# Threshold attention and a hard-swish MLP on one core: idle transposes, the relay of the score bursts, the spread of the block transposes, and the last slot's output tile

## The chip, the cores and the metric

The kernel runs on one core of a Trainium2 chip. The metric is the device time of one execution in microseconds (us). Three runs of the kernel before the change gave 502.87, 503.57 and 503.82, a median of 503.57. A separate, profiled execution is what all rows of the profile come from; its own time is given below.

The engines are named as in the profile: PE is the tensor engine (PEld its weight loads), DVE the vector engine, ACT the scalar engine, POOL is GpSimd, SP is the sync engine, which only issues DMAs and waits.

## The reference

```python
# q, k, v: (batch 8, heads 8, sequence 576, head width 64) float32, tau = 0.02
scores = q @ k.T / 8
scores = where(scores >= max(scores, -1) - tau, scores, -1e9)
attn   = softmax(scores)            # over the keys
a      = attn @ v                   # (8, 8, 576, 64)
x      = a.transpose(0, 2, 1, 3).reshape(4608, 512)
h      = x @ w_in                   # w_in: 512 x 2048
g      = h * clip(h + 3, 0, 6) / 6
out    = g @ w_out                  # w_out: 2048 x 512, out: 4608 x 512 float32
```

Attention keeps only the keys whose score lies within tau of the row's maximum; the result, laid out token by token, goes through a two-layer MLP.

## The kernel before, in words

**Slots.** The attention is cut into 144 slots, 18 for each of 8 batches (`queue`). A slot is 128 query rows of two heads. A "quad" is half of a batch's heads (4 heads), 16 quads in all. For each quad the kernel loads `nq` and `nk` (queries and keys, 576 KB each) and turns them into `qT` and `kT` with block transposes on DVE: `transpose_k` in two parts (two instructions each, L111) and `transpose_q` in two parts (one instruction each, L97). `nat_pool` keeps two buffers, so a quad's load waits until the transposes of the quad two before it have read the old one.

**One slot's softmax.** PE multiplies the scores into PSUM, for two slots together, in a `burst` (L218). DVE's `sm_max` (L232, two instructions a slot) copies them to SBUF as tile `s` and takes the row maxima; POOL makes a bias of them (L241); ACT masks (`sm_mask`, L246) and exponentiates with a row sum (`sm_exp`, L251), two instructions each; DVE takes the reciprocal (L254); POOL scales into `pn` (`sm_norm`, L259). `pn` is then transposed, for the first 10 slots by PE with copies by DVE (`pe_transpose`, L279 to L281), for all later ones by a DMA transpose on SP's queue (L270). `av` (L288) multiplies by v, a DVE copy (L296) makes `xT`, `mm1` (L311) multiplies by `w_in`, `mm1_relu` (ACT L329 or DVE L331) and `mm1_gate` (DVE L344) make g, and `mm2_part` (L311) multiplies by `w_out` in four parts a tile of 128 tokens; `mm2_out` (L363 on DVE, L361 on ACT) scales it and the output DMA goes out.

**PSUM.** There is one PSUM tile of 8 banks, divided by hand. The scores of two consecutive slots lie in banks 0 to 5 and overlap in one bank, so a burst can start only when `sm_max` has read the pair before. Banks 6 and 7 (`HB`, `OB`) serve `mm1` and `mm2`, and `pe_transpose` in the first slots.

**The relay.** Inside a burst the last products of the second slot must not start before an earlier one has ended. The wait goes over a `nop` on another engine: it waits for the matmul and releases the next ones.

```python
            if step is None:
                relay = by.nop()
                behind(relay, mm)
                continue
```

Engines work in the order of the program, so whatever stands behind the `nop` on the engine `by` waits too. In the lead-in (slots 0 to 13, two slots a cycle, loop over `n = 0, 2, ... 12`) `by` is POOL for the first cycle and DVE for the others; later it is POOL.

**Order.** Everything is written out by hand (`manual_schedule`); each engine works strictly through its own list. `at(jobs, n, ...)` puts a block transpose behind slot n's work on DVE, `at(issues, n, ...)` an input DMA at the end of slot n. Quads 2 and 3 are loaded by SP, later ones by POOL. After the lead-in each slot does its softmax, one `mm1` item, and from slot 21 on (`N2`) each odd slot two parts of `mm2` (`second()`). Behind the last slot comes the tail: `rest1` runs the `mm1` items that are left over four PSUM banks (0, 3, 2, 5 in turn), `rest2` the `mm2` tiles that are left, then come the last four `av` products, their eight `mm1` items and two more `mm2` tiles, the second in two halves (`last_tile`, L575, L578).

**Idle transposes.** `warm_up(count)` (L156) makes PE transpose an identity matrix `count` times into PSUM that nobody reads. It stands before the first burst (24), behind it (6), behind the next ones (10, then 3 a cycle) and in a few early slots (4).

Of the kernel before, what the change touches and what calls it, by code (L numbers as in the profile page):

```python
# [9 lines left out]
F32 = mybir.dt.float32  # L10
# [5 lines left out]
P = 128  # L16
# [4 lines left out]
def kernel(  # L21
# [10 lines left out]
    nc = tc.nc  # L32
    B, H, S, D = q.shape
# [6 lines left out]
    N1, N2 = 14, 21  # L40
    HB, OB = 6, 7
    R, T = 32, S // 32
# [4 lines left out]
    nat_pool = ctx.enter_context(tc.tile_pool(name="nat", bufs=2))  # L47
# [15 lines left out]
    ps = ps_pool.tile([P, 8, 512], F32, name="ps")  # L63
    ps_flat = ps[:].rearrange("p b c -> p (b c)")

    nat = {}
# [9 lines left out]
    def at(when, n, job):  # L76
        when.setdefault(n, []).append(job)
# [2 lines left out]

    def load(quad, of, t0=0, t1=T, by=nc.sync):
        b, g = divmod(quad, 2)
        if quad not in nat:
            nat[quad] = (nat_pool.tile([P, T * D], F32, tag="nq", name="nq"),
                         nat_pool.tile([P, T * D], F32, tag="nk", name="nk"))
        src = (q, k)[of][b, 4 * g:4 * g + 4].rearrange("h (r t) d -> (h r) (t d)", r=R)
        by.dma_start(out=nat[quad][of][:, t0 * D:t1 * D], in_=src[:, t0 * D:t1 * D])

    def qk_of(quad):
        if quad not in qkT:  # L90
            qkT[quad] = (qk_pool.tile([P, 2, S], F32, tag="qT", name="qT"),
                         qk_pool.tile([P, 2, S], F32, tag="kT", name="kT"))
        return qkT[quad]

    def transpose_q(quad, t0, t1):
        rows = nat[quad][0][:].rearrange("p (t j w) -> p t j w", j=2, w=32)
        nc.vector.transpose(out=qk_of(quad)[0][:].rearrange("p j (t w) -> p t j w", w=32)[:, t0:t1],  # L97
                            in_=rows[:, t0:t1])

# [1 line left out]

    def transpose_k(quad, part):
        first, e = ((0, 5), (10, 4))[part]
        rows = nat[quad][1][:].rearrange("p (t j w) -> p j t w", j=2, w=32)
        outs = qk_of(quad)[1]
        for j in range(2):
            for_u = rows[:, j, first:first + 2 * e].rearrange("p (u e) w -> p u e w", u=2)
            base = outs[:, j, :]
            o = base[:, 64 * part:64 * part + 64].rearrange("p (u w) -> p u w", u=2)
            o = bass.AP(tensor=o.tensor, offset=o.offset, ap=[list(o.ap[0]), [32, 2], [128, e], [1, 32]])  # L110
            last = nc.vector.transpose(out=o, in_=for_u)  # L111
        return last
# [41 lines left out]
    def warm_up(count):  # L154
        for _ in range(count):
            nc.tensor.transpose(ps[:, OB, P:2 * P], identf[:], identf[:])  # L156
# [12 lines left out]
    now = -1  # L169
    turn = 0  # L170

    def bank():
        nonlocal turn
        turn += 1
        return ps[:, HB, 0:256] if now < N1 else ps[:, (2, 5)[turn % 2], 0:256]

    class Slot:
        pass
# [3 lines left out]
    queue = []  # L182
# [12 lines left out]
    def score_col(n, a):  # L195
        return (512 - OWN if n % 2 else 1024 - P) + 1536 * a

    def behind(one, other):
        tc.add_manual_dep(one.ins, other.ins.name, mybir.DependencyInfo(
            mybir.DependencyClass.Sync, mybir.DependencyReason.DATA), reason="bank")  # L200

    def burst(n, by=nc.gpsimd):
        steps = ((0, 0, P, 0), (1, 0, OWN, 0), (0, 0, P, 1), None,
                 (0, P, OWN, 0), (1, 0, OWN, 1), (0, P, OWN, 1), (1, OWN, P, 0), (1, OWN, P, 1))
        for step in steps:
# [4 lines that stand above are left out]
            i, k0, w, j = step  # L210
            sl = queue[n + i]
            for a in range(2):
                c = 32 * (2 * i + a)
                c0 = score_col(n + i, a) + k0
                for quad, rows, q0 in (((2 * sl.b + sl.g, slice(0, P), sl.t * P),) if sl.t < 4 else
                                       [(2 * sl.b + g, slice(64 * g, 64 * g + 64), 512) for g in range(2)]):
                    qT, kT = qkT[quad]
                    mm = nc.tensor.matmul(ps_flat[rows, c0:c0 + w],  # L218
                                          qT[c:c + 32, j, q0:q0 + rows.stop - rows.start],
                                          kT[c:c + 32, j, k0:k0 + w], start=(j == 0), stop=(j == 1))  # L220
                    if (i, k0) == (1, OWN):
                        behind(mm, relay)
# [30 lines left out]
    def sm_recip(sl):  # L253
        nc.vector.reciprocal(out=sl.rinv[:], in_=sl.rsum[:])  # L254
# [96 lines left out]
    def mm2_part(mt, part, ob=OB):  # L351
        if part == 0:
            o_ps[0] = ps[:, ob, :]
        for ni in range(part * 4, part * 4 + 4):
            half_columns(o_ps[0], gbuf[:, ni, mt * P:(mt + 1) * P], w_out_sb[:, ni, :],
                         start=(ni == 0), stop=(ni == NI - 1))
# [15 lines left out]
    todo2 = []  # L372
# [43 lines left out]
    for quad in range(2, 2 * B):  # L416
        b, g = divmod(quad, 2)
        n0 = (b - 1) * NSLOT
        when = (((4, 5), (8, 9))[g] if b == 1 else ((-1, 1), (7, 9))[g])
        for n, of in zip(when, (1, 0)):  # L420
            at(issues, n0 + n, lambda quad=quad, of=of: load(quad, of, by=nc.sync if quad < 4 else nc.gpsimd))
        when = (8, 10, 12, 14) if quad == 2 else ((4, 6, 8, 10), (12, 14, 16, 18))[g]
        for n, job in zip(when, (lambda quad=quad: transpose_k(quad, 0), lambda quad=quad: transpose_k(quad, 1),
                                 lambda quad=quad: transpose_q(quad, 0, 8), lambda quad=quad: transpose_q(quad, 8, T))):
            at(jobs, n0 + n, job)
    for n, job in ((0, lambda: transpose_k(1, 0)), (0, lambda: transpose_k(1, 1)), (0, lambda: transpose_q(1, 0, 8)),
                   (2, lambda: transpose_q(0, 8, T)), (4, lambda: transpose_q(1, 8, T))):
        at(jobs, n, job)

    def v_pieces(b, slots):  # L430
# [24 lines left out]
    transpose_q(0, 0, 4)  # L455
    burst(0)
    transpose_q(0, 4, 8)
    warm_up(6)
    for i in range(2):
        sm_max(queue[i])  # L460
    for i in range(2):
# [1 line left out]

    def second():
        nonlocal pieces, bb, mt, part
        pieces = 2 if now % 2 and todo2 and now >= N2 else 0
        for _ in range(pieces):
            bb, mt, part = todo2.pop(0)
            mm2_part(mt, part)

    pieces = bb = mt = part = 0
# [3 lines left out]
    for n in range(0, N1, 2):  # L475
        now = n
        last = [queue[m] for m in (n - 2, n - 1) if m >= 0]
        ones, most = waiting
        for copy in ones:
            copy()  # L480
        for sl in last:
            sm_recip(sl)
        for copy in most[0:1]:
            copy()
        burst(n + 2, by=nc.vector if n else nc.gpsimd)
        for copy in most[1:]:
            copy()
        for job in jobs.get(n, ()):
            job()
        for sl in last:  # L490
            sm_norm(sl)
        if n == 0:
            for issue in issues[0][:4]:
                issue()
        sm_max(queue[n + 2])
        if n == 0:
            for issue in issues[0][4:]:
                issue()
        warm_up(10 if n == 0 else 3)
        for copy in multiply(n):  # L500
            copy()
        copies = [pe_transpose(sl) for sl in last if sl.on_chip]
        waiting = [[c[0] for c in copies], [c[1] for c in copies]]
        for issue in (issues.get(n, []) if n else []) + issues.get(n + 1, []):
            issue()
        sm_max(queue[n + 3])
        for m in (n, n + 1):
            for i in range(2):
                sm_exp(queue[m], i)
            for i in range(2):  # L510
                sm_mask(queue[m + 1], i)
# [5 lines left out]
    for n, sl in enumerate(queue[N1:], N1):  # L517
        now = n
# [67 lines left out]
        mm1_gate(item, h, mm1_relu(h, on_act))  # L586
        todo2.extend(then)

    def rest2():
        while todo2:  # L590
            bb, mt, part = todo2.pop(0)
            if (bb, mt) == (B // 2 - 1, 8):
                flush()
                last_tile(mt)
                todo2.clear()
                continue
            mm2_part(mt, part, ob=OB - count[1] % 2)
            if part == 3:
                flush()
                late.extend(mm2_out(bb, mt, on_act=(count[1] % 2 == 0)))  # L600
                count[1] += 1
# [3 lines left out]
    for item in todo1:  # L605
        rest1(*item)
    todo1.clear()
    rest2()
    for n in range(len(queue), len(queue) + 7):
        for copy in multiply(n):  # L610
            copy()
    for item in todo1:
        rest1(*item)
    rest2()
# [35 lines left out]
```

## Time and profile before

| | |
|---|---|
| median of three runs | 503.57 us |
| the profiled execution, its own time | 505.21 us |
| its span, first to last instruction | 503.4 us |
| PE busy | 486.0 us, 97% |
| DVE busy | 446.3 us, 89% |
| ACT busy | 442.5 us, 88% |
| POOL busy | 293.9 us, 58% |
| mean granted clock of the tensor engine | 0.993 |

The profiled execution takes 1.8 us more than its span, and 1.64 us more than the median of the runs. "Busy" for PE counts idle transposes, and matmuls overlap, so 97% is not the share of peak. A row of the timeline gives start, duration, engine, line, operation, `out<-in` with shape, the number of instructions merged in it, and in brackets how long the engine had been idle before it and what ended that. A row of the windows view gives, for a stretch of time, the busy time and number of instructions of PE, PEld, DVE, ACT and POOL, then the granted clock of the tensor engine (1.00 is full), the busy share of the DMA engines and their GB/s.

### The profile page before, as it was taken

The numbers are of one execution on the slowest core, as the hardware profiler recorded it, in microseconds if no ns is written. First come the engines' busy times: TensorE is split into PE (matmuls) and PEld (weight loads), VectorE is DVE, ScalarE is ACT, GpSimd is POOL, SyncE is SP. The second block draws the span as 40 slices with busy tenths as digits, with TensorE's granted clock in tenths as the row PEclk, the third lists the DMA queues.
The fourth block names the chain that finished last, engine by engine and source line by source line (L and its number), as shares of the span: only waits on it lengthen the run. The fifth ranks groups of instructions, "written<-read, shape, count | busy, mean of one in ns | idle before, by whom it ended". The sixth has DMA issues, their size and how long they took to land.

```text
span 503.4 us, 17360 instructions
## 1 busy us (share of the span) xinstructions
PE 486.0 (97%) x6788; PEld 359.8 (71%) x6788; DVE 446.3 (89%) x1154; ACT 442.5 (88%) x949; POOL 293.9 (58%) x536
## 2 busy tenths in 40 slices
PE   8889899989999999999999999999999999999996
PEld 7667676767777776777777776777777776776464
DVE  6789998999999999999999999999999998887243
ACT  2899999999999999999999999999999999998231
POOL 3767686666666665666666575666666565554000
PEclk9899999999999999999999999999999999999999
DMA  8897999888999899997979999998979869775421
GB/s 257 144 241 110 117 186 187 195 151 139 189 158 220 103 187 163 200 181 152 198 142 207 146 175 160 205 161 155 209 151 204 131 129 129 135 131 117 92 58 42
DMA packets 192626, 79.98 MB, mean 159 GB/s; under 512 B 171168, under 2 KB 183840, under 8 KB 192544
## 3 DMA queue, kind: packets, MB, share of 16 engines
q1 hardware_dynamic: 175216, 55.27, 64.5%
q0 software_dynamic: 16896, 23.07, 23.8%
q8 instruction: 53, 0.87, 0.7%
q10 hardware_dynamic: 432, 0.52, 0.4%
q14 instruction: 29, 0.24, 0.2%
HBM read 36.70 MB, written 9.44 MB: 92 GB/s over the span
## 4 chain that ended last, share of the span: by engine, by line
PE 84%; DVE 11%; issue 2%; POOL 1%; ACT 1%; DMA 0%; SPq 0%; DVEq 0%
PE ps L311 47%; PE ps L218 29%; PE ps L288 7%; DVE s L232 6%; DVE g L344 2%; PE ps L156 1%; DVE r L331 1%; POOL w_in_sb L137 1%; DVE kT L111 1%; POOL pn L259 1%; ACT r L329 1%; DVE xT L296 1%; DVE osb L363 1%; DVE qT L97 0%; DMA out_dram<-osb 0%
## 5 line engine op out<-in xcount | busy, mean ns | idle before, releaser
L232 DVE TENSOR_SCALAR_CACHE_REDUCE s<-ps 128x576 f32<-128x576 f32 x288 | 205.0, 749 | 17.9 <-PE ps L218 16.1
L259 POOL TENSOR_SCALAR pn<-s,rinv 128x576 bf16<-128x576 f32 x288 | 211.6, 749 | 15.9 <-DVE rinv L254 1.7
L246 ACT ACTIVATE s<-s,bias 128x576 f32<-128x576 f32 x288 | 205.7, 762 | 12.1 <-POOL bias L241 12.1
L251 ACT ACTIVATE s<-s 128x576 f32<-128x576 f32 x288 | 192.3, 671 | 0.0
L218 PE MATMUL ps<-kT,qT 32*128 32x128 f32 (+3 forms) x2560 | 169.7, 418 | 5.7 <-DVE s L232 5.6
L218 PEld LDWEIGHTS ps<-kT,qT 32*128 32x128 f32 (+1 forms) x2560 | 125.8, 176 | 50.7 <-DVE s L232 12.5
L311 PE MATMUL ps<-xT,w_in_sb 128*64 128x256 bf16 (+1 forms) x1936 | 132.8, 274 | 0.5 <-DVE xT L296 0.5
L311 PE MATMUL ps<-w_out_sb,g 128*64 128x512 bf16 (+1 forms) x1024 | 131.0, 379 | 1.1 <-DVE osb L363 1.1
L311 PEld LDWEIGHTS <-w_in_sb 128*64 128x64 bf16 (+1 forms) x1936 | 105.7, 109 | 10.3 <-issue 3.1
L241 POOL TENSOR_SCALAR bias<-m 128x2 f32<-128x2 f32 (+1 forms) x146 | 27.6, 189 | 140.6 <-DVE rinv L254 124.0
L311 PEld LDWEIGHTS <-g 128*64 128x64 bf16 (+1 forms) x1024 | 61.7, 109 | 49.2 <-issue 1.3
L344 DVE SCALAR_TENSOR_TENSOR g<-r,ps 128x512 bf16<-128x512 f32 x128 | 87.6, 684 | 9.6 <-ACT r L329 5.8
L329 ACT ACTIVATE r<-ps,three 128x512 f32<-128x512 f32 x81 | 55.6, 686 | 23.9 <-PE ps L311 23.6
L251 ACT ACTIVATION_READ_ACCUMULATOR s<-s 128x1 f32 x288 | 54.6, 189 | 0.0
L288 PEld LDWEIGHTS <-v 128*64 128x64 bf16 x960 | 41.4, 111 | 17.0 <-issue 4.9
L288 PE MATMUL ps<-pT,v 128*64 128x256 bf16 x640 | 45.5, 273 | 1.6 <-DVE s L232 1.5
L331 DVE TENSOR_SCALAR r<-ps 128x512 f32<-128x512 f32 x63 | 43.3, 688 | 0.4
L120 POOL DMA_DIRECT2D v<-in_v_dram x64 | 36.7, 575 | 10.2 <-DVE kT L111 4.5
L363 DVE TENSOR_SCALAR osb<-ps 128x512 f32<-128x512 f32 x32 | 21.9, 684 | 8.9 <-PE ps L311 8.9
L296 DVE CAST xT<-ps 128x256 bf16<-128x256 f32 x64 | 26.0, 406 | 3.9 <-PE ps L288 3.7
L111 DVE STREAM_TRANSPOSE kT<-nk 128x320 f32<-128x320 f32 (+1 forms) x64 | 26.2, 450 | 0.6 <-DMA nk<-in_k_dram 0.6
L97 DVE STREAM_TRANSPOSE qT<-nq 128x640 f32<-128x640 f32 (+2 forms) x33 | 24.7, 750 | 1.1 <-PE ps L218 1.1
(35 smaller groups left out, 171.5 us busy)
## 6 DMA issues: line engine op xcount, KB each, us to landing
out_dram<-osb SPq DMA_DIRECT2D x140, 64.0 KB, 2.4
nk<-in_k_dram POOLq DMA_DIRECT2D x12, 576.0 KB, 4.7
nq<-in_q_dram POOLq DMA_DIRECT2D x12, 576.0 KB, 5.2
v<-in_v_dram POOLq DMA_DIRECT2D x32, 80.0 KB, 3.9
v<-in_v_dram POOLq DMA_DIRECT2D x32, 64.0 KB, 4.0
w_in_sb<-in_moe_w_in_dram POOLq DMA_DIRECT2D x4, 512.0 KB, 10.7
w_out_sb<-in_moe_w_out_dram POOLq DMA_DIRECT2D x4, 512.0 KB, 6.9
pT<-pn SPq DMA_TRANSPOSE x120, 4.4
```

What stands on the lines that cost most here:

```text
L111: last = nc.vector.transpose(out=o, in_=for_u)
L120: nc.gpsimd.dma_start(out=vsb[b % 2][32 * g:32 * g + 32].rearrange("p (hp a) c -> p a hp c", a=2)[:, a, :, c0 * D:(c0 + count) * D], in_=v ...
L218: mm = nc.tensor.matmul(ps_flat[rows, c0:c0 + w], qT[c:c + 32, j, q0:q0 + rows.stop - rows.start], kT[c:c + 32, j, k0:k0 + w], start=(j == ...
L232: nc.vector.tensor_scalar(out=sl.s[:, i, :], in0=ps_flat[:, c0:c0 + S], scalar1=1.0, scalar2=None, op0=Alu.mult, op1=Alu.max, accum_out=sl ...
L246: nc.scalar.activation(out=s, in_=s, func=Act.Prelu, bias=sl.bias[:, i:i + 1], scale=scale, alpha=REJECT)
L251: nc.scalar.activation(out=s, in_=s, func=Act.Exp, accum_out=sl.rsum[:, i:i + 1])
L259: nc.gpsimd.tensor_scalar(out=pn[:, i, :], in0=sl.s[:, i, :], scalar1=sl.rinv[:, i:i + 1], scalar2=1.0, op0=Alu.mult, op1=Alu.mult)
L288: nc.tensor.matmul(pb[a * 64:(a + 1) * 64, :], vsb[b % 2][:, 2 * hp + a, u * D:(u + 1) * D], pT[:, block, cols], start=(c == 0), stop=(c = ...
L311: nc.tensor.matmul(out[c:c + w], lhsT[:, c:c + w], rhs, start=start, stop=stop)
L329: nc.scalar.activation(out=r, in_=hps, func=Act.Relu, bias=three[:])
L331: nc.vector.tensor_scalar(out=r, in0=hps, scalar1=3.0, scalar2=0.0, op0=Alu.add, op1=Alu.max)
L344: nc.vector.scalar_tensor_tensor(out=out, in0=r, scalar=6.0, in1=hps, op0=Alu.min, op1=Alu.mult)
```

## The change

Eight places are edited, in three groups.

*Lead-in.* The idle transposes behind burst 0 become 15 (6 before), in cycle 0 they become 15 (10), in cycle 2 they become 8 (3). The relays of all lead-in bursts move to SP.

*Loads and block transposes.* `nat` is kept by quad and kind, so that queries and keys take their buffers separately. On SP, the keys of quad 2 are issued in cycle 0 (in cycle 4 before), its queries stay in cycle 4, and quad 3 stays in cycle 8; with the relays on SP these issues now stand behind them in SP's list. The queries of every even quad from 4 on are issued by POOL two slots later. The second query part of quad 1 moves from cycle 4 to cycle 2. The four transposes of quad 2 move from cycles or slots 8, 10, 12, 14 to 4, 8, 12, 20, those of quad 3 from 12, 14, 16, 18 to 14, 16, 18, 22. Their number stays the same.

*Tail.* Slot 143 no longer runs two parts of a new `mm2` tile. `rest2(4)` leaves one tile's four parts over, which run behind the last four `av` products, and these products get four PSUM banks in turn, not two.

```diff
-        if quad not in nat:
-            nat[quad] = (nat_pool.tile([P, T * D], F32, tag="nq", name="nq"),
-                         nat_pool.tile([P, T * D], F32, tag="nk", name="nk"))
+        if (quad, of) not in nat:
+            nat[quad, of] = nat_pool.tile([P, T * D], F32, tag=("nq", "nk")[of], name=("nq", "nk")[of])
...
-        return ps[:, HB, 0:256] if now < N1 else ps[:, (2, 5)[turn % 2], 0:256]
+        if now < N1:
+            return ps[:, HB, 0:256]
+        return ps[:, (2, 5)[turn % 2] if now < len(queue) else (2, 5, 0, 3)[turn % 4], 0:256]
...
-        when = (((4, 5), (8, 9))[g] if b == 1 else ((-1, 1), (7, 9))[g])
+        when = (((1, 5), (8, 9))[g] if b == 1 else ((-1, 3), (7, 9))[g])
...
-        when = (8, 10, 12, 14) if quad == 2 else ((4, 6, 8, 10), (12, 14, 16, 18))[g]
+        when = (((4, 8, 12, 20), (14, 16, 18, 22)) if b == 1 else ((4, 6, 8, 10), (12, 14, 16, 18)))[g]
...
-                   (2, lambda: transpose_q(0, 8, T)), (4, lambda: transpose_q(1, 8, T))):
+                   (2, lambda: transpose_q(0, 8, T)), (2, lambda: transpose_q(1, 8, T))):
...
-    warm_up(6)
+    warm_up(15)
...
-        pieces = 2 if now % 2 and todo2 and now >= N2 else 0
+        pieces = 2 if now % 2 and todo2 and N2 <= now < len(queue) - 1 else 0
...
-        burst(n + 2, by=nc.vector if n else nc.gpsimd)
+        burst(n + 2, by=nc.sync)
...
-        warm_up(10 if n == 0 else 3)
+        warm_up({0: 15, 2: 8}.get(n, 3))
...
-    def rest2():
-        while todo2:
+    def rest2(leave=0):
+        while len(todo2) > leave:
...
-    rest2()
-    for n in range(len(queue), len(queue) + 7):
+    rest2(4)
+    now = len(queue)
+    for n in range(now, now + 7):
         for copy in multiply(n):
             copy()
+    rest2()
```

More of the change, by code (lines that the diff above doesn't have):

```diff
@@ L82, in load @@
         b, g = divmod(quad, 2)
-        if quad not in nat:
-            nat[quad] = (nat_pool.tile([P, T * D], F32, tag="nq", name="nq"),
-                         nat_pool.tile([P, T * D], F32, tag="nk", name="nk"))
+        if (quad, of) not in nat:
+            nat[quad, of] = nat_pool.tile([P, T * D], F32, tag=("nq", "nk")[of], name=("nq", "nk")[of])
         src = (q, k)[of][b, 4 * g:4 * g + 4].rearrange("h (r t) d -> (h r) (t d)", r=R)
-        by.dma_start(out=nat[quad][of][:, t0 * D:t1 * D], in_=src[:, t0 * D:t1 * D])
+        by.dma_start(out=nat[quad, of][:, t0 * D:t1 * D], in_=src[:, t0 * D:t1 * D])
     def qk_of(quad):
@@ L95, in transpose_q @@
     def transpose_q(quad, t0, t1):
-        rows = nat[quad][0][:].rearrange("p (t j w) -> p t j w", j=2, w=32)
+        rows = nat[quad, 0][:].rearrange("p (t j w) -> p t j w", j=2, w=32)
         nc.vector.transpose(out=qk_of(quad)[0][:].rearrange("p j (t w) -> p t j w", w=32)[:, t0:t1],
@@ L103, in transpose_k @@
         first, e = ((0, 5), (10, 4))[part]
-        rows = nat[quad][1][:].rearrange("p (t j w) -> p j t w", j=2, w=32)
+        rows = nat[quad, 1][:].rearrange("p (t j w) -> p j t w", j=2, w=32)
         outs = qk_of(quad)[1]
```

## The prediction

> **What bounds the kernel now.** I read the page first: who is busy, and when the clock was down.
>
> ```profile
> PE 486.0 (97%) x6788; PEld 359.8 (71%) x6788; DVE 446.3 (89%) x1154; ACT 442.5 (88%) x949; POOL 293.9 (58%) x536
> PEclk9899999999999999999999999999999999999999
> PE 84%; DVE 11%; issue 2%; POOL 1%; ACT 1%; DMA 0%; SPq 0%; DVEq 0%
> ```
>
> PE carries the chain. From 200 to 400 us the windows view gives it no idle time at all, and in that stretch the change does nothing but move one load per even quad. So a microsecond gained before slot 22 or so arrives at the end undiminished, as does one gained behind the last slot. The lead-in is another matter: there DVE, PE and ACT wait for each other. The waits of the first 100 us show it:
>
> ```profile
> ACT s L246 <- POOL bias L241: 12.1, 9, 7.8
> PEld ps L218 <- DVE s L232: 8.6, 20, 1.7
> DVE s L232 <- PE ps L218: 7.3, 8, 2.6
> ```
>
> (us in total, times, longest.) A burst needs the previous pair's maxima, and the maxima need the burst. The page's clock row has an 8 in its second slice (12.6 to 25.2 us), so I cut these slices into microseconds in the windows view:
>
> ```profile
> 13.00:14.00 1.00, 1.00 (x15) 0.72 (x9) 1.00 (x3) 1.00 (x3) 0.32 (x1) 0.68 0.10 20
> 15.00:16.00 1.00, 1.00 (x6) 1.00 (x7) 1.00 (x3) 0.67 (x2) 0.86 (x2) 0.50 0.95 106
> 16.00:17.00 1.00, 1.00 (x6) 0.83 (x4) 1.00 (x3) 0.25 (x1) 0.41 (x2) 0.61 1.07 124
> 23.00:24.00 1.00, 0.86 (x11) 0.76 (x15) 0.63 (x7) 0.60 (x1) 0.47 (x3) 0.80 1.21 274
> 25.00:26.00 1.00, 1.00 (x12) 0.52 (x7) 0.45 (x1) 1.00 (x4) 1.00 (x2) 0.50 1.09 327
> 27.00:28.00 1.00, 1.00 (x18) 0.87 (x13) 0.40 (x1) 1.00 (x3) 0.00 (x0) 0.99 1.09 306
> ```
>
> The clock (third number from the end) was at half from 13.36 (0.64 of the first row at half, 0.36 at full) to 16.78, and from 23.6 to 27.0: two stretches of 3.4 us, on a grid of 3.4 us. In the grid interval before the first, 9.95 to 13.37, PE worked about 1.9 us (55%); before the second, 20.2 to 23.6, about 2.1 us (62%). In 27.0 to 30.4 it worked 78% and nothing followed. The price stands in the timeline:
>
> ```profile
> 8.98 0.88 PE L156 MATMUL ps<-identf 128*128 128x128 f32 x6
> 11.99 2.92 PE L218 MATMUL ps<-kT,qT 32*128 32x128 f32 x30 [0.20 <-DVE s L232]
> 15.00 0.76 DVE L232 TENSOR_SCALAR_CACHE_REDUCE s<-ps 128x576 f32<-128x576 f32 x1 [1.00 <-PE ps L218]
> 17.85 2.22 PE L218 MATMUL ps<-kT,qT 32*128 32x128 f32 x30 [0.20 <-DVE s L232]
> 19.07 0.85 DVE L97 STREAM_TRANSPOSE qT<-nq 128x640 f32<-128x640 f32 x1 [1.14 <-PE ps L218]
> 23.52 3.92 PE L218 MATMUL ps<-kT,qT 32*128 32x128 f32 x32
> 27.61 0.76 DVE L232 TENSOR_SCALAR_CACHE_REDUCE s<-ps 128x576 f32<-128x576 f32 x1 [0.61 <-POOL pn L259]
> 52.20 0.82 PE L288 MATMUL ps<-pR,v 128*64 128x64 bf16 x40 [1.34 <-DVE s L232]
> ```
>
> The same 30 matmuls took 2.92 and 2.22 us, and DVE waited behind the slow ones (it names POOL at 27.61, but the burst had only just ended). At 19.07 DVE waits in the relay; at 52.20 PE waits because DVE has a heavy cycle. The tail has two gaps:
>
> ```profile
> 457.22 1.89 PE L311 MATMUL ps<-w_out_sb,g 128*128 128x512 bf16 x8 [1.13 <-DVE osb L363]
> 485.45 7.15 PE L311 MATMUL ps<-xT,w_in_sb 128*128 128x256 bf16 x64 [0.52 <-DVE xT L296]
> ```
>
> **The change part by part.** I follow the cycles by the moment the second slot's maxima are done: 17.71, 23.04, 30.32, 35.89, 41.69, 47.35 and 53.74 us.
>
> *15 idle transposes behind burst 0.* At full clock they cost 0.11 us each (three in 0.55 us, six in 0.88), so 15 end at 8.98 + 1.87 = 10.85; burst 2 starts at 11.31 by DVE's maxima. Hidden, and the idle 1.45 us shrinks to 0.46. The interval 9.95 to 13.37 then holds 2.7 us of work, 79%, like the interval that was not answered by half clock. With that stretch gone burst 2 ends at 11.99 + 2.22, the maxima begin at 14.30 instead of 15.00: **0.7 us** gained. DVE's transposes to 14.00 cover no more. In other executions the grid lies elsewhere, and 0 to 0.7 is the bound.
>
> Do idle transposes count as work at all? The 24 at the start took 5.12 us, 0.213 each, half clock, and nothing else ran on PE from 1.8 to 6.8; burst 0 behind them ran 32 matmuls in 2.23 us, full clock. So they counted. [...]
>
> *15 in cycle 0, 8 in cycle 2.* At full clock: 14.2 + 1.9 = 16.1 and burst 4 is due at 16.5: hidden. At half clock 15 × 0.213 = 3.2 us, to 18.1, against 17.17 now: up to 0.9 us late. The eight end near 20.4, when PE waits for POOL's `pn` anyway (four steps of 0.73 us set the pace): at most 0.1. They and the shift of 0.7 lift the second interval from 62% to some 75%. Between a refused 62% and an allowed 78% I take the nearer. Then burst 6 takes 2.3 us, not 3.92, and ends at 25.85; DVE has, from 23.04, 0.87 (copies, reciprocals), 1.34 (two copies) and 0.9 (a key transpose, in place of the query transpose of 0.84 that goes to cycle 2), which is 26.15. Against 27.61: **1.46 us** gained, bounds 0 to 1.5.
>
> *Relays on SP.* DVE no longer waits 1.14 (cycle 2), 0.98 (cycle 4) and 0.3 us (later cycles), but the next maxima wait for the same burst's end anyway. So alone it is worth nothing; it makes room of some 0.75 us a cycle for a block transpose. In cycle 2 two query transposes, 1.7 us, now end at 23.04 − 4.1 = 18.95, before the burst's end at 19.4: hidden. POOL's v issues start 1.5 us earlier; its next bias waits for DVE regardless. Queued behind a relay on SP: the loads of quads 2 and 3. The keys of quad 2 go from 5.83 to about 12.5 us; landing takes 6.8 us, use is at 24.5, cover 5 us. The others land more than 8 us ahead. If that cover went, cycle 4 would pay it one for one. A relay on SP costs what the POOL's does, not visible in the rows of bursts, ±0.2.
>
> *Fewer transposes in late cycles.* Cycles without surplus are paced by burst plus maxima: 5.57 us (30.32 to 35.89). Cycle 8 took 5.80, cycle 10 5.66 and cycle 12, with two transpose jobs (0.70, 0.86), 6.39. After: 0.76, none, 0.70, each inside the 0.75 us. Gain 0.2 + 0.1 + 0.8 = **1.1 us**. ACT needs 2.66 a slot, 5.32 a cycle, so it follows.
>
> *What comes back in slots 14 to 22.* Slot 14 loses 0.68 us of DVE work, slots 20 and 22 get 0.84 each. DVE idled 0.68 us at 74.00 and 1.24 at 80.07, waiting for bursts in just these slots; so 0.16 and 0 remain. ACT's 0.2 us wait at 58.67 goes. Net 0, bounds −0.2 to +0.8.
>
> *Tail.* Without the new tile PE does not wait 1.13 us for `osb`. But the eight matmuls had filled a time in which ACT still had the last slot's exponentials, to 459.83. PE's `mm1` items now start at 456.05, 0.87 each; the fourth needs bank 0, which the gate frees at 459.2, the fifth bank 3, whose relu starts at 459.85 and whose gate ends at 461.26. Waits: 459.35 − 458.66 = 0.69 and 461.4 − 460.22 = 1.18, together 1.87. So 0.74 is lost here. Later the leftover tile covers the `xT` copies: 0.52 gained. **Net +0.2 us**, bounds −0.5 to +0.9, without a clock drop.
>
> *Sum.* 0.7 + 1.46 + 1.1 − 0.2 = 3.1 us, from the profiled 505.21 to 502.1. The median lies 1.64 lower, and I cannot tell whether its runs had both half-clock stretches. If so 500.5; if neither, only 1.1 − 0.2 is left, 502.7. I take three quarters of the clock terms (1.5 of 2.16): 503.57 − 2.4 = **501.2**.
>
> **The rivals.**
>
> *The clock terms don't come.* The gap intervals stay under the gate's limit, or the median's runs had no half-clock stretch to lose. Against: the filled interval stands at 79%. For: the grid. [...] Time: 502.6 to 502.9.
>
> *The tail trips the gate.* PE's 1.87 us of idle time lie between 458.66 and 461.4; in one interval of 3.4 us that leaves 45%, under both refused ones, and half clock follows for 3.4 us: up to 1.7 us lost while PE works without a pause. Against: the interval must hold both gaps, 0.7 of 3.4 positions; with one gap it stays at 65% or more. It turns the sign only where the lead-in gives under 1.9 us: 503.57 − 1.1 + 0.2 + 1.7 = 504.4.
>
> *Room elsewhere.* The cycles run below 5.57 us because the bursts wait less: 499.8.
>
> **How the numbers follow.** Some 0.2% (1.0 us) is what a measurement of this kernel can tell from no change. Forecast, 500.2 to 502.4: 0.63, all faster. Clock terms absent, 502.4 to 503.5: 0.19, of which 0.04 is faster and 0.15 the same. The tail's half clock: 0.14, of which 0.03 ends within 0.2% and 0.11 slower, about 504. Better than 500.2: 0.04. So faster 0.71, same 0.18, slower 0.11. The range, 499.9 to 503.6, leaves out most of the tail case and little else.
>
> **What would show it.** Right: no half clock between 10 and 30 us, cycle 4 in about 5.8 us instead of 7.28, cycle 12 in 5.6 instead of 6.39, the first exponential of slot 14 near 50.7 us (53.80 before), PE gaps of 0.7 and 1.2 us at the last slot's `mm1` items, none before the last eight. Wrong: a half-clock row in 10 to 30 us or at the tail, DVE waiting for `nk`, or PE idle in slots 20 to 24.

## The result, and the profile after

The changed kernel takes 500.94 us (median of six runs, 500.80 to 501.23). The kernel before, run beside it, took 503.69 (six runs, 502.87 to 505.23). The ratio is 0.9943, with a 95% interval from 0.9928 to 0.9959: faster by 2.75 us. The forecast was 501.2. The profiled execution of the changed kernel took 501.12 us, its span 499.4, against 505.21 and 503.4. That pair differs by 4.1 us, more than the medians do; why is shown with the experiments.

The page of the changed kernel, the same three rows as before (busy times, clock, chain by engine):

```profile
PE 484.4 (97%) x6803; PEld 359.3 (72%) x6807; DVE 446.0 (89%) x1154; ACT 441.5 (88%) x949; POOL 294.1 (59%) x536
PEclk9999999999999999999999999999999999999999
PE 79%; ACT 12%; DVE 6%; issue 1%; POOL 1%; DMA 0%; SPq 0%; DVEq 0%
```

The dip in the clock row is gone. ACT has 12% of the chain, where it had 1%; the windows view further down shows why. The waits of the first 100 us:

```profile
ACT s L247 <- POOL bias L242: 9.4, 4, 7.9
PEld ps L219 <- DVE s L233: 8.5, 22, 0.8
DVE s L233 <- PE ps L219: 4.3, 6, 1.7
```

ACT waits 2.7 us less, and DVE waits 3.0 us less for bursts. The rows of the timeline that answer those shown before (lines are one higher here: L155 idle transposes, L219 bursts, L233 maxima, L96 query transposes):

```profile
9.09 1.86 PE L155 MATMUL ps<-identf 128*128 128x128 f32 x15
12.10 2.22 PE L219 MATMUL ps<-kT,qT 32*128 32x128 f32 x30 [0.20 <-DVE s L233]
14.40 0.76 DVE L233 TENSOR_SCALAR_CACHE_REDUCE s<-ps 128x576 f32<-128x576 f32 x1 [0.29 <-PE ps L219]
17.25 1.55 DVE L96 STREAM_TRANSPOSE qT<-nq 128x640 f32<-128x640 f32 x2
22.93 2.23 PE L219 MATMUL ps<-kT,qT 32*128 32x128 f32 x32
25.34 0.76 DVE L233 TENSOR_SCALAR_CACHE_REDUCE s<-ps 128x576 f32<-128x576 f32 x1
48.77 0.82 PE L289 MATMUL ps<-pR,v 128*64 128x64 bf16 x40 [0.51 <-DVE s L233]
```

The 15 idle transposes take 1.86 us and are over before the next burst. Burst 2's matmuls take 2.22 us (2.92 before), burst 6 takes 2.23 (3.92 before), and DVE no longer stops in a relay (1.14 us at 19.07 before): its two query transposes follow the reciprocals at once. PE's wait before the `av` products at 48.77 is 0.51 us, where it was 1.34. The wait that the prediction named as a sign of being wrong, DVE for `nk`, occurs once, 0.89 us at 4.53 us, for the very first keys; before it was 0.61. The first exponential of slot 14 starts at 50.79 us (forecast 50.7). The cycles, measured as in the prediction by the end of the second slot's maxima:

| cycle | 0 | 2 | 4 | 6 | 8 | 10 | 12 | then slot 16 |
|---|---|---|---|---|---|---|---|---|
| before, us | 5.86 | 5.33 | 7.28 | 5.57 | 5.80 | 5.66 | 6.39 | 5.95 |
| after, us | 5.15 | 5.33 | 5.61 | 5.57 | 5.56 | 5.57 | 5.56 | 5.35 |
| before at full clock (`fill_only`, below), us | 5.15 | 5.42 | 5.76 | 5.57 | 5.79 | 5.67 | 6.39 | 5.94 |

"Then slot 16" is the time from slot 15's maxima to slot 17's. Slot 15's maxima are done 3.43 us earlier than before, slot 17's 4.03, slot 21's 3.66. From there the lead stays: 3.64 at slots 23 to 71 and 3.73 at slot 143. So what was gained in the lead-in did arrive at the end.

### The profile page after: what moved, and what is told of

Its sections match the earlier page's. It is cut to its first block, busy times and chain, and to the rows that moved or that the text cites. A ratio compares the mean times of both kernels' runs of the same rounds, so it can differ in the third digit from the quotient of the medians.

```text
span 499.4 us, 17393 instructions
## 1 busy us (share of the span) xinstructions
PE 484.4 (97%) x6803; PEld 359.3 (72%) x6807; DVE 446.0 (89%) x1154; ACT 441.5 (88%) x949; POOL 294.1 (59%) x536
## 4 chain that ended last, share of the span: by engine, by line
PE 79%; ACT 12%; DVE 6%; issue 1%; POOL 1%; DMA 0%; SPq 0%; DVEq 0%
PE ps L312 45%; PE ps L219 26%; PE ps L289 6%; ACT s L247 5%; ACT s L252 5%; DVE s L233 4%; ACT r L330 1%; DVE g L345 1%; PE ps L155 1%; POOL w_in_sb L136 1%; DMA out_dram<-osb 0%; POOL pn L260 0%; DVE r L332 0%; DVE osb L364 0%; PE ps L159 0%
## 5 line engine op out<-in xcount | busy, mean ns | idle before, releaser
L233 DVE TENSOR_SCALAR_CACHE_REDUCE s<-ps 128x576 f32<-128x576 f32 x288 | 205.2, 750 | 16.3 <-PE ps L219 12.9
L219 PE MATMUL ps<-kT,qT 32*128 32x128 f32 (+3 forms) x2560 | 167.3, 414 | 4.8 <-DVE s L233 4.4
L219 PEld LDWEIGHTS ps<-kT,qT 32*128 32x128 f32 (+1 forms) x2560 | 124.1, 174 | 49.2 <-DVE s L233 11.1
L96 DVE STREAM_TRANSPOSE qT<-nq 128x640 f32<-128x640 f32 (+2 forms) x33 | 24.6, 749 | 0.6 <-DMA nq<-in_q_dram 0.6
```

What stands on the lines that cost most here:

```text
L219: mm = nc.tensor.matmul(ps_flat[rows, c0:c0 + w], qT[c:c + 32, j, q0:q0 + rows.stop - rows.start], kT[c:c + 32, j, k0:k0 + w], start=(j == ...
L233: nc.vector.tensor_scalar(out=sl.s[:, i, :], in0=ps_flat[:, c0:c0 + S], scalar1=1.0, scalar2=None, op0=Alu.mult, op1=Alu.max, accum_out=sl ...
```

## The experiments

Every run lists its mean granted clock, and in this kernel that number counts half-clock stretches. One stretch of 3.41 us at half clock takes 1.7 us of some 500, or 0.0034, off the mean; two take 0.0068. A stretch that begins behind PE's last matmul takes up to 0.002 off and costs nothing (in the profile of the changed kernel, mean 0.999, the clock falls at 498.28 us, and PE's last matmul ends at 495.55). So 0.998 to 1.000 means none while PE works, 0.995 to 0.997 one, and 0.994 and less two or more. The kernel before was run 74 times beside the experiments, on three chips:

| half-clock stretches | runs of 74 | median, us | range, us |
|---|---|---|---|
| none | 35 | 502.97 | 502.55 to 503.28 |
| one | 29 | 504.18 | 503.63 to 504.74 |
| two | 10 | 505.23 | 505.04 to 505.76 |

The profiled execution of before was one of the ten. The price fits the prediction's 0.7 and 1.46 us, 2.16 together: measured 2.26 between none and two. But the median of before, 503.69, lies only 0.72 us above the runs with none, about the price of the first stretch alone.

**Idle transposes as before in the changed kernel (old_fill).**

```diff
-    warm_up(15)
+    warm_up(6)
...
-        warm_up({0: 15, 2: 8}.get(n, 3))
+        warm_up(10 if n == 0 else 3)
```

> The changed kernel with the idle transposes of before (6, 10, 3). Theory (they keep the clock up): half-clock stretches come back between 10 and 30 us in some or all runs, and cost 0.7 us in cycle 0 and 1.5 to 1.7 us in cycle 4 where they do; the median goes from 500.9 up by about 1.3 to 502.2, and runs spread by 1 us or more. Rival (idle transposes do not count as work, the gain is from relays and spread): 500.9, within 0.3.

Measured: 502.29 us. Eight of twelve runs had a stretch or two (0.993 to 0.996, 502.2 to 503.05 us), four had none, and these took 500.73 to 501.19, the changed kernel's time. The theory held.

**New idle transposes alone (fill_only).** The reverse of that diff on the kernel before.

> The kernel before with the idle transposes of the change alone (15, 15, 8). Theory: no half clock between 10 and 30 us, 1.3 us less than before (503.7), so 502.4, and runs that spread by no more than 0.5 us. Rival (they do not count as work): 503.7, or up to 0.9 later where 15 transposes at half clock hold up the next burst.

Measured: 502.90 us (502.56 to 503.23), no stretch in twelve runs. So the edit removes the stretches, as the theory had it, but its worth at the median is 0.8 us and not 1.3. Beside the 35 runs of before without a stretch, 502.97, the new idle transposes change nothing: they are the clock's price and no more. Its profile is therefore the kernel before at full clock, and stands in the table of the cycles: cycle 0 takes 5.15 us there, cycle 4 takes 5.76. So 1.52 of the 1.67 us that cycle 4 lost are the clock's.

**No idle transposes behind burst 0 and in cycles 0 and 2 (no_fill).** The changed kernel without them:

```diff
-    warm_up(15)
+    warm_up(0)
...
-        warm_up({0: 15, 2: 8}.get(n, 3))
+        warm_up({0: 0, 2: 0}.get(n, 3))
```

> The changed kernel without any idle transposes behind burst 0 and in cycles 0 and 2. Theory: PE's idle share between 9 and 24 us grows, half clock returns in every run, and the median goes up by 2 to 3 us from 500.9 to about 503.3. Rival (they do not count as work): 500.9 or less, since nothing stands before the bursts.

Measured: 502.89 us, 1.95 more than the changed kernel, and a stretch in all twelve runs. Its bursts 2 and 4 in the timeline:

```profile
11.69 3.71 PE L219 MATMUL ps<-kT,qT 32*128 32x128 f32 x30 [0.16 <-DVE s L233]
18.32 3.81 PE L219 MATMUL ps<-kT,qT 32*128 32x128 f32 x30 [0.19 <-DVE s L233]
```

The 30 matmuls that take 2.22 us at full clock take 3.71 and 3.81. Fewer instructions on the busiest engine made the kernel slower.

**Each filler by itself (fill_first, fill_later).** The first keeps 15 behind burst 0 and takes 10 and 3 in the cycles; the second keeps 6 behind burst 0 and takes 15 and 8.

> The changed kernel with 15 idle transposes behind burst 0, but 10 and 3 in cycles 0 and 2 as before. Theory (each gap of PE has its own half-clock stretch): no stretch from the first gap; one from the gaps in cycle 2 in some of the runs, at 1.4 us each; those runs near 502.4, the others at 501.0. Rival (one filler is enough for both): 501.0 in all runs.

> The changed kernel with 6 idle transposes behind burst 0 as before, but 15 and 8 in cycles 0 and 2. Theory: one half-clock stretch from the first gap in some of the runs, at 0.7 us, or up to 1.7 where 15 transposes at half clock hold up burst 4; those near 501.7 to 502.6, the others at 501.0. Rival (one filler is enough for both): 501.0 in all runs.

Measured: fill_first 501.15 us, five runs of six without a stretch (500.95 to 501.25), one with (502.46). fill_later 501.93, eight runs of eleven with one stretch (501.72 to 502.44), three without (500.76 to 501.11). Each gap has its own stretch, as expected. With the first gap open the stretch came in eight of eleven runs, with only the later ones open in one of six.

**Relays (dve_relay, sp_relay_only).** The changed kernel with the relays of before, and the kernel before with the relays on SP:

```diff
-        burst(n + 2, by=nc.sync)
+        burst(n + 2, by=nc.vector if n else nc.gpsimd)
```

> The changed kernel with the relays of before (POOL in cycle 0, DVE later). Theory (relays on SP are worth only the room for block transposes): cycle 2 is 0.5 us longer, because two query transposes stand behind the relay and end near 20.0 us, and cycles 4, 8 and 12 by 0.2 each; 502.0. Rival (the relay's place is worth nothing here either): 500.9.

> The kernel before with its relays on SP alone. Theory: 503.7, within 0.4, since the next maxima wait for the same burst; the cycles with one transpose lose 0.1 to 0.3 us each at most. Rival (DVE's waits in the relay, 1.14 and 0.98 us, are on the path): 502.0 or less.

Measured: dve_relay 501.07 us, 0.13 from the changed kernel; its cycle 2 did grow by 0.21, but not the 1.1 us in sum that I expected. sp_relay_only 503.22, and its five runs without a stretch took 501.91 to 502.08, median 502.04. That is 0.93 below before's 502.97, and near the rival. Its cycles 8, 10 and 12 took 5.56, 5.57 and 6.01 us, 0.71 less in sum than at full clock before; cycles 2 and 4 (5.32 and 5.60) give another 0.26.

**Block transposes and loads alone (spread_only).** The kernel before with the change's two lists of slots, the moved query part of quad 1 and the separate buffers; relays, idle transposes and tail as before.

> The kernel before with the loads and block transposes of the change alone (relays, idle transposes and tail as before). Theory: cycle 12 gains 0.8 us, cycles 8 and 10 0.1 to 0.3, cycle 2 loses up to 0.5 behind the relay; about 503.1. Rival (the spread needs no relay): 502.6.

Measured: 502.81 us; five of twelve runs were without a stretch and took 501.22 to 501.61, median 501.33. That is 1.64 below before's 502.97 (1.81 below the 503.14 of before's full-clock runs on the same chip), far more than expected. So at full clock the relays alone are worth 0.93, the spread alone 1.64, and both together (with the old tail: old_tail below, 501.19) 1.78. They don't add up, because either one shortens the same thing, a DVE list longer than the burst beside it, and because ACT is the next floor. The windows view of before (first fence) and of the changed kernel, between 24 and 62 us (columns after the length: PE, PEld, DVE, ACT, POOL busy):

```profile
24.00:34.00 10.00, 9.22 (x135) 6.61 (x129) 7.66 (x20) 9.39 (x21) 7.01 (x11) 0.85 1.15 284
44.00:54.00 10.00, 8.12 (x139) 6.49 (x139) 9.71 (x32) 8.81 (x20) 6.52 (x13) 1.00 0.87 124
```

```profile
24.00:34.00 10.00, 8.73 (x144) 6.34 (x140) 9.15 (x30) 10.00 (x24) 7.62 (x14) 1.00 1.11 216
44.00:54.00 10.00, 9.29 (x157) 7.48 (x154) 9.74 (x30) 10.00 (x23) 7.57 (x14) 1.00 0.94 136
54.00:62.00 8.00, 7.87 (x109) 6.23 (x107) 7.74 (x24) 8.00 (x20) 5.44 (x12) 1.00 0.91 136
```

ACT is busy 9.39, 8.81 of 10 us before, and without a gap after. From 24.15 us on its exponentials come every 2.66 us up to slot 14. Two slots are 5.32 us and a cycle is 5.57, so ACT lives on a backlog there, and no further relief of DVE can shorten this stretch of ACT's work. The times from one slot's first row sum on ACT to the next show what DVE's surplus cost at full clock. From slot 4 to slot 13 they are 2.66 us in `fill_only` as well, so the longer cycles 8 and 10 did not reach ACT; only two steps are longer:

| step on ACT, us | slot 13 to 14 | slot 15 to 16 |
|---|---|---|
| `fill_only` | 3.57 | 3.54 |
| `sp_relay_only` | 2.71 | 3.55 |
| `spread_only` | 2.66 | 3.24 |
| changed kernel | 2.66 | 3.24 |

The spread alone already frees both, and the relays alone nearly all of the first. These steps hold 1.21 of the 1.78 us; where each part of the rest lies was not separated.

**One transpose moved out of slot 14 (late_q2).** dve_relay with the transposes where they were before, but the second query part of quad 2 in slot 20.

```diff
-        when = (((4, 8, 12, 20), (14, 16, 18, 22)) if b == 1 else ((4, 6, 8, 10), (12, 14, 16, 18)))[g]
+        when = (((8, 10, 12, 20), (12, 14, 16, 18)) if b == 1 else ((4, 6, 8, 10), (12, 14, 16, 18)))[g]
...
-                   (2, lambda: transpose_q(0, 8, T)), (2, lambda: transpose_q(1, 8, T))):
+                   (2, lambda: transpose_q(0, 8, T)), (4, lambda: transpose_q(1, 8, T))):
```

> The changed kernel with the relays of before and the block transposes and their places of before, but for one: the second query part of quad 2 goes from slot 14 to slot 20. Idle transposes and tail as changed. Theory (DVE's surplus in slot 14 was on the path by itself): the interval from slot 15's maxima to slot 17's falls from 5.95 to 5.35 us, while cycle 12 stays at 6.39; 502.90 for idle transposes alone, less 0.27 for the tail, less 0.6: 502.0. Rival (the 0.6 us there came only from the lighter cycle 12): 502.6.

Measured: 502.39 us, between the two. The interval to slot 17 did fall to 5.32 with cycle 12 at 6.40, so slot 14's surplus was on the path by itself. But 0.39 us came back from slot 19 to slot 21 (6.27 us, 5.88 in fill_only and before). On ACT the gain is smaller from the start: the step from slot 15 to 16 falls from 3.54 to 3.24 us, 0.30, and the runs give 502.90 − 0.25 (the tail, below) − 502.39 = 0.26. The changed kernel gives 0.37 back between slots 17 and 21 as well, dve_relay only 0.06. In the changed kernel's rows DVE has got ahead of ACT there, waits for its relu, and the burst waits for the copy behind it; dve_relay has neither wait:

```profile
61.39 0.69 DVE L345 SCALAR_TENSOR_TENSOR g<-r,ps 128x512 bf16<-128x512 f32 x1 [0.22 <-ACT r L330]
62.52 1.77 PE L219 MATMUL ps<-kT,qT 32*128 32x448 f32 x20 [0.28 <-DVE xT L297]
```

For late_q2 the profile names no such wait (its maxima start 0.33 us late with no releaser shown), and no run tests it; this stays open.

**The tail (old_tail, tail_bank).** The changed kernel with the tail of before, and a version of my own: the new tile stays in the last slot, but in bank 4, which is free there, and the `mm1` items left over take five banks. The leftover tile of the change stays too. The diff is that of tail_bank:

```diff
-        pieces = 2 if now % 2 and todo2 and N2 <= now < len(queue) - 1 else 0
+        pieces = 2 if now % 2 and todo2 and now >= N2 else 0
...
-            mm2_part(mt, part)
+            mm2_part(mt, part, ob=4 if now == len(queue) - 1 else OB)
...
-        h = mm1(item, hb=(0, 3, 2, 5)[count[0] % 4])
+        h = mm1(item, hb=(0, 3, 2, 5, 1)[count[0] % 5])
```

> The changed kernel with the tail of before (a new output tile in the last slot, nothing left over, two banks). Theory from the two traces (the tail gained 0.27 us): 501.2. The prediction's sum (the tail loses 0.2 us): 500.7.

> The changed kernel with the new output tile back in the last slot, but in bank 4, which nobody reads there, and the leftover mm1 items over five banks (0, 3, 2, 5, 1); the leftover tile stays. Theory (PE waits 1.43 us for gates there only because nothing else is in its list): the waits go, 499.5. Rival (ACT's chain of relus sets the pace anyway and the wait comes back behind the items): 500.9.

Measured: old_tail 501.19 us, so the change's tail is worth some 0.25 us. That is no more than the spread of the runs (500.80 to 501.23 and 501.01 to 501.42), but the traces agree: the changed kernel is 3.73 us ahead of before at slot 143's maxima and 4.00 at the last eight items, and from those maxima to the start of its last `mm2` matmuls it takes 41.02 us, old_tail 41.28 and before 41.29. tail_bank 499.38 (499.16 to 499.54; ratio to before 0.9919, interval 0.9905 to 0.9933), 1.56 less than the changed kernel and the fastest version here. The changed kernel's tail in its timeline has PE waiting for gates, and no wait before the last items:

```profile
455.55 1.03 PE L312 MATMUL ps<-xT,w_in_sb 128*128 128x256 bf16 x8 [0.56 <-DVE g L345]
457.45 1.03 PE L312 MATMUL ps<-xT,w_in_sb 128*128 128x256 bf16 x8 [0.87 <-DVE g L345]
481.45 7.15 PE L312 MATMUL ps<-xT,w_in_sb 128*128 128x256 bf16 x64
```

In tail_bank these waits are gone. The same stretch from slot 143's maxima takes 39.27 us. The eight matmuls of the new tile (second row) follow the last slot's item at once, and the 40 of the leftover items follow them. How much bank 4 and the fifth bank each give was not run apart.

```profile
450.03 2.02 PE L312 MATMUL ps<-xT,w_in_sb 128*64 128x256 bf16 x24
451.89 1.89 PE L312 MATMUL ps<-w_out_sb,g 128*128 128x512 bf16 x8
453.62 4.53 PE L312 MATMUL ps<-xT,w_in_sb 128*128 128x256 bf16 x40
```

There are two kinds of filler, then: matmuls that had to be done anyway, here, and transposes of nothing, at the start.

## Why the prediction was right, and where it was not

The forecast of 2.4 us met 2.75 with the right sign, and the clock, relays and spread were the right causes. But the closeness is luck: the clock term was too large, the others were too small, and the tail had the wrong sign.

*The clock, mechanism right, share too large.* With the gaps filled the clock stayed up: no stretch in twelve runs of fill_only, against eight of twelve in old_fill and twelve of twelve in no_fill. The prices from one profile held: cycle 0 fell by 0.71 us (forecast 0.7), cycle 4 by 1.67, of which 1.52 are the clock's (forecast 1.46). The step that failed is "I take three quarters of the clock terms (1.5 of 2.16)" for the median; three quarters would be 1.62, and the median of before loses 0.72 us. The profiled execution happened to be the worst of three kinds, and with it I had only three times, none of which said which kind it was.

*Where the grid lies.* The 24 idle transposes at the start take 0.213 us each in before, against 0.11 at full clock (in the changed kernel 15 take 1.86 us and 8 take 1.09), and burst 0 behind them is at full clock, with 32 matmuls in 2.23 us. The granted clock of the windows view reads 1.00 from 0 to 5 us, so only the durations tell. I read their total as showing when full speed began. In the profiles of before, fill_only and the changed kernel, in this order:

```profile
1.77 5.12 PE L156 MATMUL ps<-identf 128*128 128x128 f32 x24
```

```profile
1.77 3.76 PE L156 MATMUL ps<-identf 128*128 128x128 f32 x24
```

```profile
1.77 5.22 PE L155 MATMUL ps<-identf 128*128 128x128 f32 x24
```

The same instructions from the same start take 3.76 to 5.22 us, so the moment of full speed is not tied to the kernel's start. The stretches show the grid: in before the two begin at 13.37 and 23.60 us, 10.23 apart, three times 3.41. In the six profiles that have a half-clock stretch the total goes with the grid:

| | before | fill_later | old_fill | spread_only | sp_relay_only | no_fill |
|---|---|---|---|---|---|---|
| 24 idle transposes, us | 5.12 | 5.09 | 4.56 | 4.54 | 4.28 | 4.12 |
| first half-clock stretch begins at, us | 13.37 | 13.31 | 12.22 | 12.18 | 11.64 | 11.32 |

A grid that lies 1 us later makes the 24 transposes 0.49 us longer (between no_fill and before 1.00 for 2.05), as it must if each takes 0.213 us ahead of the switch and 0.11 behind it. I take the place of the grid to be the reason why some runs of before had a stretch and others none; before has no kept trace of a run without one. These float32 transposes counted as work: in fill_only, where the 24 took 3.76 us and not the 5.11 of 24 at 0.213, full speed came while they were still running, and PE had done nothing else but the two blank products before 2 us. With the 15, 15 and 8 left out a stretch came in twelve runs of twelve, with them in none of the changed kernel's six.

*Relays and spread, 1.1 us forecast, 1.78 at full clock.* The late cycles gave 0.24 + 0.09 + 0.83 = 1.16 in the traces, as summed. Cycles 2 and 4 gave 0.09 and 0.15 more at full clock (against `fill_only`), which the sum did not have. Two steps failed. "alone it is worth nothing" for the relays: alone they gave 0.93, because a cycle with a transpose had no room to spare while DVE also stood in the relay; the prediction put that room to the spread's account only. And "Net 0" for slots 14 to 22: the lighter slot 14 gave 0.6 us by the interval, of which 0.37 came back by slot 21. I had named the 0.68 us that slot 14 loses, and still put the net at nothing; only the upper bound, 0.8, allowed for it.

*Tail, −0.2 forecast, +0.25 measured.* The waits were where I put them, behind banks 0 and 3, but 0.56 and 0.87 us, not 0.69 and 1.18: the items' modelled ends overlap (the item at 457.45 us is listed with 1.03 us, and the next matmuls start 0.87 behind it), so I counted a latency as idle. By the starts of the rows, from the last slot's items to the first leftover `mm2` matmul PE lost 0.49 us (forecast 0.74): 461.78 − 450.34 plus eight matmuls of 0.217 is 13.18, against 12.69 before. The cover for the `xT` copies gave 0.74 (forecast 0.52): 5.77 less 16 matmuls of 0.216, 2.31, against 3.05 before.

So the non-clock terms, forecast 0.9, are 502.97 − 500.94 = 2.03 us, and the clock terms, forecast 1.5, are 0.72. The sums nearly agree; the split did not.

*Rivals.* Half of the first came true, the clock term being worth half of what I took for the median, but the rest was underrated. The second, a half-clock stretch in the tail, did not happen: of 24 runs with the changed tail and all the new idle transposes (the changed kernel, dve_relay, late_q2) none shows one while PE works. Why not is open: by the windows view the two gaps of 0.56 and 0.87 us still leave PE 58% busy in some positions of an interval of 3.41 us (1.98 us from 454.50).

## What to carry to other kernels

Before you price a stall from one profile, find out whether every run has it: the granted clock sorted 74 runs of one kernel into three groups that the median alone hides. Here useless work made an engine faster: the 30 matmuls of burst 2 took 2.22 us with it and 3.71 without. It was over before the next real work was due, and no run tests what it costs where it is not. Useful work that was already in the engine's list is better, and free PSUM banks may be all it takes to put it there (tail_bank, 1.56 us). Edits that relieve the same engine can be substitutes (here 0.93 and 1.64 us alone, 1.78 together): cost them together, against the engine that becomes the floor next.

## What the runs showed of the hardware that was not expected

Half clock did not need a long gap. In before it followed intervals of 3.41 us in which PE worked 54 and 61%, with no gap over 1.5 us in them. The kept traces have eight such stretches, and the busy shares before them are 34, 34, 51, 52, 54, 54, 55 and 61%. Intervals of the same grid with 65% (spread_only, from 15.59 us), 66% (sp_relay_only, from 15.05) and 68% (old_fill, from 15.63) were not followed by one, nor was one of before with 61 to 62% (2.07 to 2.12 us from 50.85 to 50.91 us, counted on from 13.37). So half clock followed shares of up to 61% of busy time as the profile counts it (2.06 us between 20.20 and 23.60 in before, which the prediction took for 62%), and these four from 61 to 68% were without it; the prediction had only 78 there. The changed kernel's two intervals hold 80% (from 10.16 us) and 73% (from 20.40), if its grid lies 0.20 us behind that of before, as 5.22 against 5.12 us for the 24 transposes would have it. That a share of busy time is the whole rule is not shown: the tail, with 58% in some positions, had no stretch.
